# Windowed attention and a squared-ReLU MLP in one program: fp32 transposes, casting DMAs, hand-written engine orders, and products with V in 64-column array tiles

## The chip, the cores and the metric

The program runs on one core of one Trainium2 chip. The metric is device time in microseconds for one execution. TensorE (PE; its weight loads are shown as PEld), VectorE (DVE), ScalarE (ACT), GpSimd (POOL) and SyncE (SP) each run their own queue of instructions in order, and wait for each other through semaphores. DMA transfers are issued from a queue of SP, ACT or POOL.

## The reference

Attention over 8 batches, 8 heads, 576 positions and 64 values per head. A query sees the keys within 32 positions, and 8 global positions, drawn at random, see all and are seen by all. Its output, 4,608 tokens of 512 values, goes through two matrix products with a scaled and shifted squared ReLU between them.

```python
scores = scale * np.matmul(q, k.transpose(0, 1, 3, 2))
mask = np.abs(pos[:, None] - pos[None, :]) <= 32
mask = mask | is_global[:, None] | is_global[None, :]
scores = np.where(mask, scores, -1e9)
attn = softmax(scores)            # over the keys
x = np.matmul(attn, v)            # [8, 8, 576, 64] -> tokens [4608, 512]
r = np.maximum(x @ w_in, 0.0)     # w_in [512, 2048]
out = (s * (r * r) + b) @ w_out   # w_out [2048, 512]
```

## The kernel before

A batch's 576 positions are cut into five chunks of 120 (the last has 96); each chunk is filled to 128 rows with the 8 global positions. So a band of neighbouring chunks and the 8 globals cover everything a query can see, and a query that is global gets its sums from all five chunks (`gs`, and `finish_batch`, which writes its columns into `xt` at positions read from registers, one POOL copy per global, L398).

Heads are taken in pairs; pair p is heads 2hp and 2hp+1 of batch bi, with p = 4 bi + hp, so there are 32 pairs. For each pair: five transposes of K and five of Q (`trans_k`, `trans_q`) turn the natural rows into `kt` and into `qbufs`, where the two heads lie block-diagonally, with zeros in the other blocks. `qk` makes one score matrix per chunk for both heads at once, ScalarE takes its exponential, VectorE multiplies it with a mask. `pv` multiplies with V; `vbufs` holds 64 columns of V and 64 of ones beside them, so that a head's product has its output on partitions 0 to 63 and its row sums, 64 times over, on 64 to 127, and the two heads follow one another along the free dimension of `po`. `norm` takes the logarithm and the exponential of minus that (the reciprocal) on 64 partitions and 1,280 columns, and multiplies once per head.

The MLP runs in quanta of 0.9 us or so: a block of 512 tokens has 16 for the first product (4 weight tiles each, ReLU on ScalarE, square on VectorE) and 16 for the second. They are put between the attention steps by `Q`, eight per pair, as soon as a batch of attention is done; 32 quanta become due per batch and 64 after the last.

K, Q and V are loaded in fp32 by SP in halves of four heads (`load`, L124). The rows of the globals are gathered once for all batches by 24 DMAs on ACT's queue into a scratch in DRAM and copied from there into every chunk (`fill_globals`). Then casts to bf16 follow, on VectorE and POOL for batch 0 and on POOL afterwards (L285 to L287). The MLP weights are loaded in fp32 and cast, scaled by `s` and summed on POOL (`load_w`). PE's and SP's orders are as written; for ACT, DVE and POOL a scheduler of the framework sets the order:

```python
    ctx.enter_context(tc.manual_schedule(engines={ET.PE, ET.SP}))
```

Of the kernel before, what the change touches and what calls it, by code (L numbers as in the profile page):

```python
# [9 lines left out]
FP32 = mybir.dt.float32  # L10
# [22 lines left out]
W = [HI[c] - LO[c] for c in range(NCH)]  # L33

# [8 lines left out]

def halves(ap):

    return bass.AP(
        tensor=ap.tensor, offset=ap.offset,
        ap=[list(ap.ap[0]), [P, NCH], [HB + NG, 2], [1, HB]],
    )
# [3 lines left out]
def kernel(  # L53
# [14 lines left out]
    ctx.enter_context(tc.manual_schedule(engines={ET.PE, ET.SP}))  # L68
# [3 lines left out]
    natp = ctx.enter_context(tc.tile_pool(name="natp", bufs=1))  # L72
    castp = ctx.enter_context(tc.tile_pool(name="castp", bufs=2))
# [5 lines left out]
    mop = ctx.enter_context(tc.tile_pool(name="mop", bufs=3))  # L79
    dramp = ctx.enter_context(tc.tile_pool(name="dramp", bufs=1, space=bass.MemoryType.DRAM))  # L80
# [23 lines left out]
    nat = {}  # L104
    NATSRC = {"k": k, "q": q, "v": v}
    HG = 4

    def nat_tile(t, half):
        key = (t, half)
        if key not in nat:  # L110
            nat[key] = natp.tile([P, NCH, HG, D], FP32, tag=f"nat{t}{half}", name=f"nat{t}{half}")
        return nat[key]

    for t in ("k", "q", "v"):
        for half in range(2):
            nc.gpsimd.memset(nat_tile(t, half)[96:P, NCH - 1], 0.0)

    def load(bi, t, h0, nh):
        src = NATSRC[t]
        d = nat_tile(t, h0 // HG)  # L120
        a = h0 % HG
        for c in range(NCH):
            n = min(KC, S - KC * c)
            nc.sync.dma_start(  # L124
                out=d[0:n, c, a : a + nh],
                in_=src[bi, h0 : h0 + nh, KC * c : KC * c + n].rearrange("h s d -> s h d"),
            )

    gsc = {
        t: dramp.tile([B, NG, H, D], FP32, name=f"gsc{t}", tag=f"gsc{t}")  # L130
        for t in ("k", "q", "v")
    }

    def gather(eng, t, regs):
        for i in range(NG):
            eng.dma_start(
                out=gsc[t][:, i], in_=NATSRC[t][:, :, ds(regs[i], 1), :].rearrange("b h o d -> b (h o) d")
            )

    def fill_globals(eng, bi, t, half):  # L140
        d = nat_tile(t, half)
        src = gsc[t][bi, :, HG * half : HG * half + HG].rearrange("g h d -> g (h d)")
        src = bass.AP(
            tensor=src.tensor, offset=src.offset,
            ap=[list(src.ap[0]), [0, NCH], list(src.ap[1])],
        )
        eng.dma_start(
            out=d[KC:P].rearrange("p c h d -> p c (h d)"), in_=src
        )

    greg_a = [
        nc.scalar.value_load(g32[:1, i, 0:1], min_val=0, max_val=S - 1) for i in range(NG)
    ]
    greg_p = [
        nc.gpsimd.value_load(g32[:1, i, 0:1], min_val=0, max_val=S - 1) for i in range(NG)
    ]
    for t in ("k", "q", "v"):
        gather(nc.scalar, t, greg_a)

    for half in range(2):  # L160
        for t in ("k", "q", "v"):
            load(0, t, HG * half, HG)
            fill_globals(nc.scalar, 0, t, half)


    s_bc = const.tile([P, 1], FP32)
    nc.sync.dma_start(out=s_bc[:], in_=_bcast_dram(moe_s[:], P))
    b_bc = const.tile([P, 1], FP32)
    nc.sync.dma_start(out=b_bc[:], in_=_bcast_dram(moe_b[:], P))
    win_t = wpool.tile([P, 4, DF], BF16)  # L170
# [216 lines left out]
    def finish_batch(bi):  # L387
# [9 lines left out]
        for i in range(NG):  # L397
            nc.gpsimd.tensor_copy(  # L398
                out=xt[:, :, ds(greg_p[i], 1)], in_=xg[:, :, i : i + 1]
            )  # L400


    gts = {}
    gpb = {}

    def moe_quanta():
# [156 lines left out]
```

## Time and profile before

| | |
|---|---|
| median of 3 runs | 484.63 us (483.41 to 487.75) |
| the profiled execution | 487.77 us, with a span of 486.0 us from its first to its last instruction |
| PE, DVE, ACT, POOL busy | 73%, 60%, 47%, 27% of the span |
| first transpose; first product with V | 46.37 us; 68.76 us |
| ends of the batches' first and last `po` tiles | batch 0: 70 to 98 us; batch 7: 391 to 418 us |
| last stretch without attention | 424.2 to 486.0 us |
| DMA | 48.99 MB, mean 101 GB/s |

A row of a group reads: line, engine, operation, tiles out<-in, shapes, count; then total busy us and mean ns of one; then the idle time before these instructions and who ended it. In a timeline the first two numbers are the start and the duration in us, and a bracket gives the idle time before the row and its releaser. In the chain of waits the rows are start, duration and what ran. PEclk is the clock that TensorE was granted, as a share of full speed.

### The profile page before, as it was taken

To read this page: it belongs to the slowest core of one execution; us is meant where nothing else is said; L and a number is where in the kernel's file an instruction comes from. 1 tells how busy PE (TensorE), PEld (TensorE's weight loads), DVE (VectorE), ACT (ScalarE), POOL (GpSimd) and SP (SyncE) were. 2 spreads that over 40 slices of the span, in tenths; PEclk is the share of its full clock that TensorE was granted. 3 is DMA by queue.
4 is the path that set the end of the run, shared out by engine and by line. 5 is a ranking of instruction groups with operands and counts; after the bars stand their busy time and mean duration, and the time that the engine had idled before them with its cause. 6 is when DMAs were issued, how large, how long until landed. Compare 5 with 4: busy or idle time off the path is not lost.

```text
span 486.0 us, 7310 instructions
## 1 busy us (share of the span) xinstructions
PE 353.8 (73%) x2503; PEld 212.4 (44%) x2530; DVE 293.5 (60%) x672; ACT 230.8 (47%) x369; POOL 129.8 (27%) x155
## 2 busy tenths in 40 slices
PE   0000325558996897699969979996999599699996
PEld 0000113324553553366547537754765375354442
DVE  3902908849865865467758666775776476533331
ACT  1000115436844763387448645853865486352340
POOL 4334999934006200420241024024000100100000
PEclk9999999999997998799989998998999899989999
DMA  7999159999913105960990695199001000100102
GB/s 122 187 296 219 41 187 185 167 165 167 170 21 76 42 1 98 169 135 1 191 197 13 109 170 123 38 180 183 1 35 54 22 1 23 65 1 29 59 10 78
DMA packets 128149, 48.99 MB, mean 101 GB/s; under 512 B 117488, under 2 KB 119408, under 8 KB 128112
## 3 DMA queue, kind: packets, MB, share of 16 engines
q1 hardware_dynamic: 126096, 47.89, 50.7%
q10 hardware_dynamic: 2016, 0.64, 0.8%
q8 instruction: 20, 0.33, 0.3%
q14 instruction: 17, 0.14, 0.1%
HBM read 39.07 MB, written 9.83 MB: 101 GB/s over the span
## 4 chain that ended last, share of the span: by engine, by line
PE 34%; issue 26%; POOL 10%; DMA 10%; ACT 7%; SPq 6%; DVE 5%; ACTq 1%; POOLq 1%; DVEq 0%
PE psh L421 17%; PE pso L436 11%; SPq L124 5%; PE po L357 3%; ACT r L428 3%; POOL wout_t L470 2%; POOL xt L398 2%; DMA wi<-in_moe_w_in_dram 2%; ACT rep L374 2%; PE pss L334 2%; POOL wsum L477 2%; DMA wo<-in_moe_w_out_dram 2%; DVE xt L381 2%; POOL qb L286 2%; DMA natq<-in_q_dram 1%
## 5 line engine op out<-in xcount | busy, mean ns | idle before, releaser
L421 PE MATMUL psh<-xt,win_t 128*128 128x512 bf16 (+7 forms) x1020 | 155.7, 303 | 41.5 <-POOL xt L398 37.2
L436 PE MATMUL pso<-wout_t,g 128*128 128x512 bf16 x553 | 137.9, 382 | 4.7 <-DVE osb L443 3.3
L421 PEld LDWEIGHTS <-win_t 128*128 128x128 bf16 x1024 | 91.6, 103 | 95.4 <-issue 57.9
L428 ACT ACTIVATE r<-psh 128x512 bf16<-128x512 f32 x144 | 86.4, 600 | 87.3 <-PE psh L421 81.9
L338 ACT ACTIVATE e<-pss 128x384 bf16<-128x384 f32 (+1 forms) x160 | 73.4, 471 | 79.7 <-DMA wo<-in_moe_w_out_dram 49.5
L430 DVE TENSOR_TENSOR g<-r 128x512 bf16<-128x512 bf16 x144 | 70.6, 490 | 62.5 <-ACT r L428 62.1
L436 PEld LDWEIGHTS <-g 128*128 128x128 bf16 x576 | 55.6, 98 | 65.2 <-issue 10.1
L340 DVE TENSOR_TENSOR em<-e,mask 128x384 bf16<-128x384 bf16 (+1 forms) x160 | 73.1, 477 | 8.0 <-ACT e L338 6.9
L372 ACT ACTIVATE ln<-po 64x1280 f32<-64x1280 f32 x32 | 39.4, 1232 | 69.7 <-PE po L357 69.7
L334 PE MATMUL pss<-qbd,kt 128*128 128x384 bf16 (+1 forms) x160 | 55.1, 352 | 12.0 <-ACT e L338 9.9
L381 DVE TENSOR_TENSOR xt<-po,rep 64x600 bf16<-64x600 f32 x64 | 49.6, 775 | 16.3 <-ACT rep L374 14.8
L398 POOL COPY xt<-xg 128x4 bf16 x64 | 13.9, 217 | 145.0 <-DVE xt L381 102.7
L300 PE MATMUL pst<-ident,kb 128*128 128x128 bf16 x160 | 15.4, 232 | 48.3 <-DVE kb L285 46.4
L357 PE MATMUL po<-em,vx 128*128 128x160 bf16 (+3 forms) x448 | 35.7, 228 | 17.7 <-POOL vx L287 12.1
L285 POOL CAST kb<-natk 128x1280 bf16<-128x1280 f32 x14 | 18.0, 1284 | 100.4 <-DMA natq<-gscq 55.9
L374 ACT ACTIVATE rep<-ln 64x1280 f32<-64x1280 f32 x32 | 40.5, 1267 | 0.9
L443 DVE TENSOR_TENSOR osb<-pso,bias_row 128x512 f32<-128x512 f32 x36 | 24.7, 690 | 22.8 <-PE pso L436 22.5
L357 PEld LDWEIGHTS <-vx 128*128 128x128 bf16 x448 | 29.3, 101 | 19.5 <-POOL vx L287 12.3
L318 DVE COPY qbd<-pst 64x600 bf16<-64x600 bf16 x64 | 29.9, 466 | 11.8 <-PE pst L312 11.4
L300 PEld LDWEIGHTS <-kb 128*128 128x128 bf16 x160 | 12.2, 103 | 55.2 <-DVE kb L285 46.4
L375 DVE TENSOR_REDUCE gs<-po 128x16 f32<-128x80 f32 x32 | 7.7, 241 | 33.1 <-ACT ln L372 33.0
L334 PEld LDWEIGHTS <-kt 128*128 128x128 bf16 x160 | 16.5, 105 | 24.7 <-issue 12.1
(56 smaller groups left out, 190.3 us busy)
## 6 DMA issues: line engine op xcount, KB each, us to landing
out_dram<-osb SPq DMA_DIRECT2D x36, 256.0 KB
natk<-in_k_dram SPq DMA_DIRECT2D x64, 120.0 KB
natq<-in_q_dram SPq DMA_DIRECT2D x64, 120.0 KB
natv<-in_v_dram SPq DMA_DIRECT2D x64, 120.0 KB
wi<-in_moe_w_in_dram SPq DMA_DIRECT2D x4, 1024.0 KB
wo<-in_moe_w_out_dram SPq DMA_DIRECT2D x4, 1024.0 KB
natk<-in_k_dram SPq DMA_DIRECT2D x16, 96.0 KB
natq<-in_q_dram SPq DMA_DIRECT2D x16, 96.0 KB
```

What stands on the lines that cost most here:

```text
L318: nc.vector.tensor_copy(out=halves(qt[r, hh]), in_=ps[r].rearrange("p (c j) -> p c j", c=NCH)[:, :, 0:KC].rearrange("p c (a j) -> p c a j" ...
L334: nc.tensor.matmul(ps[:], kt[:, P * c : P * c + P], qt[:, :, LO[c] : HI[c]])
L338: nc.scalar.activation(e[:], ps[:], AF.Exp, scale=SCALE)
L340: nc.vector.tensor_mul(em[:], e[:], masks[c][:])
L357: nc.tensor.matmul(po[:, a : a + n], vx[:, c, 2 * hp + hh, :], emt[(p, c)][:, hh, lo - LO[c] : lo - LO[c] + n], start=bank not in started, ...
L372: nc.scalar.activation(ln[D:P], po[D:P], AF.Ln)
L374: nc.scalar.activation(rep[D:P], ln[D:P], AF.Exp, scale=-1.0)
L381: nc.vector.tensor_tensor(out=xt[D * hh : D * hh + D, hp].rearrange("p (c a j) -> p c a j", c=NCH, a=2), in0=halves(po[0:D, hh * LQ : hh * ...
L421: nc.tensor.matmul(psh[:, d0 : d0 + n], win_t[:, a, f * P : f * P + P], xts[bi][:, a, x0 : x0 + n], start=(a == 0 and j == 0), stop=(a == ...
L428: nc.scalar.activation(r[:], psh[:], AF.Relu)
L430: nc.vector.tensor_mul(g[:], r[:], r[:])
L436: nc.tensor.matmul(pso[:], gl[f][:, u * P : u * P + P], wout_t[:, f], start=(f == 0), stop=(f == 15),)
```

## The change

**Precision and layout of the inputs.** K and Q stay in fp32 and are transposed as fp32, with an fp32 identity. The copy out of PSUM makes the bf16. The eight rows of the globals now lie first in a chunk of K and V, and between the two halves of 60 in a chunk of Q, where `qbufs` has them, so that plain copies suffice. V and `w_in` are cast by the DMA that loads them, issued from POOL. `w_out` is copied to bf16 by ScalarE and its rows summed by VectorE, and `s` is applied when a tile is stored. K, Q and V have two buffers, each for all eight heads.

**Globals of batch 0.** They don't come through DRAM any more: fp32 products with a selection matrix take them out of the loaded rows (`select_globals`, `select_v`). The gathers for the other batches are issued from POOL after pair 0 and pair 1.

**Order.** All five engines' orders are as written. A pair has eight slots. VectorE's part of a slot is put off to the next one (`later`), and the normalising of a pair is done in slots 1 and 3 of the next pair. `finish_batch` comes in slot 5 of the next batch's first pair and is issued in slot 6. Batch 0 runs without quanta, then 14 quanta go beside `weights_out`, then batch 1 has three quanta per pair and each later batch 8 per pair; six quanta of a block are always left over when the next block becomes due.

**Products with V.** `pv` writes the products of the two heads to partitions 0 to 63 and 64 to 127 of the same columns, with 64 columns of weights each: first the V columns of both heads (`part` 0), then the ones (`part` 1). So the row sums of both heads stand on 128 partitions in 640 columns, and there is one logarithm, one exponential and one multiply per pair at 128 partitions. There are 28 products per pair where there were 14.

```diff
-    ctx.enter_context(tc.manual_schedule(engines={ET.PE, ET.SP}))
+    ctx.enter_context(
+        tc.manual_schedule(engines={ET.PE, ET.SP, ET.Activation, ET.DVE, ET.Pool})
+    )
...
+    def load_v(bi):
+        d = vbufs[bi % 2]
+        for c in range(NCH):
+            n = min(KC, S - KC * c)
+            nc.gpsimd.dma_start(
+                out=d[NG : NG + n, c, :, 0:D],
+                in_=v[bi, :, KC * c : KC * c + n].rearrange("h s d -> s h d"),
+            )
+
+    load_k(nc.sync, 0, 0, HG)
+    load_q(nc.scalar, 0, 0, HG, 0)
+    load_q(nc.sync, 0, 0, HG, 1)
+    load_v(0)
...
+    for j in range(4):
+        nc.gpsimd.dma_start(
+            out=win_t[:, :, 512 * j : 512 * j + 512],
+            in_=w_in2[:, :, 512 * j : 512 * j + 512],
+        )
...
+    def tr(ps, dst0, src, c, hp):
+        nc.tensor.transpose(
+            ps[:, dst0 : dst0 + P], src2(src)[:, c, P * hp : P * hp + P], identf[:]
+        )
...
+    def trans_a(p):
+        bi, hp = divmod(p, 4)
+        ps = ps_s.tile([P, 512], FP32, tag="s", name="pst")
+        for c in range(4):
+            tr(ps, P * c, natk[bi % 2], c, hp)
+        kt = ktp.tile([P, LQ], BF16, tag="kt", name="kt")
+        ktile[p] = kt
+        nc.scalar.copy(out=kt[:, 0:512], in_=ps[:])
...
+        for i, (src, sel) in enumerate(((natk[0], selk), (natq[0], selq))):
+            for c in range(NCH):
+                nc.tensor.matmul(
+                    ps[:, i], src2(src)[:, c, P * hp : P * hp + P], sel[:, c],
+                    start=(c == 0), stop=(c == NCH - 1),
+                )
...
     def pv(p):
         bi, hp = divmod(p, 4)
-        vx = vbufs[bi % NV]
+        vx = vbufs[bi % 2]
         po = ps_o.tile([P, 2 * LQ], FP32, tag="o", name="po")
         started = set()
-        for hh in range(2):
+        for part in range(2):
             for c in range(NCH):
...
+                for a, n, x in pieces(part * LQ, c):
+                    for hh in range(2):
+                        key = (a // 512, hh)
+                        nc.tensor.matmul(
+                            po[D * hh : D * hh + D, a : a + n],
+                            vx[:, c, 2 * hp + hh, D * part : D * part + D],
+                            emt[(p, c)][:, hh, x : x + n],
+                            start=key not in started, stop=(part == 1 or c == NCH - 1),
+                            skip_group_check=True,
+                        )
+                        started.add(key)
...
-        nc.scalar.activation(ln[D:P], po[D:P], AF.Ln)
...
+            nc.scalar.activation(ln[:], po[:, LQ : 2 * LQ], AF.Ln)
...
+        for s in range(8):
+            prev, later[:] = list(later), []
+            if s < NCH:
+                qk(p, s)
+                if s in (1, 3, 4):
+                    step()
+            elif s == 5:
+                if hp == 0 and bi > 0:
+                    later.append(lambda: finish_batch(bi - 1))
+                if trans_next:
+                    trans_a(p + 1)
+            elif s == 6:
+                if trans_next:
+                    trans_b(p + 1)
+                    if bi == 0:
+                        select_globals(p + 1)
+            else:
+                if p == 0:
+                    select_v()
+                pv(p)
+                pending.extend(norm_steps(p))
+            for f in prev:
+                f()
+            Q(nq[s])
...
+    for p in range(4):
+        run_pair(p, Z, p < 3)
+        if p == 0:
+            gather(k, gsk)
+            gather(q, gsq)
+        if p == 1:
+            gather(v, gsv)
...
+            load_v(1)
+            prefetch_hw(1)
...
+        nq = [1] * 8 if bi > 1 else [0, 1, 0, 1, 0, 1, 0, 0]
```

Three places show how the instructions stand. On TensorE, in batch 0, from the last transpose ahead of pair 0's product with V before; `vx_401` is V with its ones, `em` the masked exponentials:

```order
L312 MATMUL pst<-ident,qb 128x128
L357 LDWEIGHTS vx_401
L357 MATMUL po<-em_527,vx_401 128x160
L357 LDWEIGHTS vx_401
L357 MATMUL po<-em_533,vx_401 128x192
```

And at the same place now, for pair 1, with the selecting products (`psg`) between:

```order
L349 MATMUL pst<-identf,natk_98 128x128 x4
L349 MATMUL pst_508<-identf,natk_98 128x128
L349 MATMUL pst_508<-identf,natq_100 128x128
L349 MATMUL pst<-identf,natq_100 128x128 x4
L391 MATMUL psg<-selk,natk_98 128x8 x5
L391 MATMUL psg<-selq,natq_100 128x8 x5
L450 LDWEIGHTS vx_102
L450 MATMUL po<-em_471,vx_102 64x160
L450 LDWEIGHTS vx_102
L450 MATMUL po<-em_471,vx_102 64x160
```

Each chunk has two products of 64 rows where it had one of 128, the transposes read the loaded fp32 tiles, and an fp32 product stands without a load row of its own.

On POOL, at the start before, where `qbd` are the tiles of `qbufs` and the casts of the weights follow them:

```order
L275 MEMSET qbd_405 64x640
L276 MEMSET qbd_405 64x640
L275 MEMSET qbd_408 64x640
L276 MEMSET qbd_408 64x640
L275 MEMSET qbd_411 64x640
L276 MEMSET qbd_411 64x640
L465 CAST win_t<-wi 128x4x512 x4
```

And now, of POOL's start, the issues and the last register load ahead of them:

```order
L170 DMA vx_102<-in_v_dram 120x8x64 x4
L170 DMA vx_102<-in_v_dram 96x8x64
L194 DMA win_t<-in_moe_w_in_dram 128x4x512 x4
L206 TENSOR_LOAD gidx_i_96
L206 ISA x2
...
L301 MEMSET qbd_104 64x640
L302 MEMSET qbd_104 64x640
```

The clearing of `qbufs` has moved behind nine DMA issues and eight register loads.

On TensorE at the end of batch 2, where the first product of a new MLP block (`psh`) reads the last columns of `xt`, before:

```order
L357 MATMUL po<-em_1978,vx_401 128x160
...
L436 LDWEIGHTS g_1777
L436 MATMUL pso<-wout_t,g_1777 128x512
L334 LDWEIGHTS kt
L334 MATMUL pss<-qbd_405,kt 128x320
L421 LDWEIGHTS win_t
L421 MATMUL psh<-xt,win_t 128x128
```

And now, in slots 4 to 6 of batch 3's first pair:

```order
L423 MATMUL pss<-qbd_104,kt 128x320
...
L349 MATMUL pst<-identf,natk_99 128x128 x4
...
L533 LDWEIGHTS g_1878
L533 MATMUL pso<-wout_t,g_1878 128x512
L349 MATMUL pst_2129<-identf,natk_99 128x128
L349 MATMUL pst_2129<-identf,natq_101 128x128
L349 MATMUL pst<-identf,natq_101 128x128 x4
L518 LDWEIGHTS win_t
L518 MATMUL psh<-xt,win_t 128x128
```

Two quanta and one score stood between the last product with V and the new block; now a whole pair's scores, its transposes and six quanta do.

More of the change, by code (lines that the diff above doesn't have):

```diff
@@ L102 @@
     g32 = gidx_i64[:].bitcast(mybir.dt.int32).rearrange("p (a b) -> p a b", b=2)
[L104 to L149, printed above, removed]
@@ L262 @@
[L262 to L274 removed]
+        if c in (0, NCH - 1):
+            nc.vector.tensor_copy(
+                out=gadd[:, WIN + HB : WIN + HB + NG], in_=view(vkey[:, c : c + 1], [0, NG])
+            )
@@ L479, in bias @@
+    flush()
+    while pending:
+        step()
+        flush()
+    finish_batch(0)
+    quanta[0] = 32
+    for j in range(4):
+        Q(3)
+        weights_out(j)
+        flush()
+    Q(2)
+    flush()
+    trans_a(4)
+    trans_b(4)
+    flush()
     def bias():
```

569 lines of the change are left out of this document (316 added, 253 removed).

## The prediction

> **What bounds the kernel now.** I read the page's span and busy shares, then the time by stage, then one batch's end, the groups by line, and last the start.
>
> ```profile
> span 486.0 us, 7310 instructions
> PE 353.8 (73%) x2503; PEld 212.4 (44%) x2530; DVE 293.5 (60%) x672; ACT 230.8 (47%) x369; POOL 129.8 (27%) x155
> ```
>
> The shares average over very different stages, so the windows come next: up to the first product with V, batch 0's pairs, batch 1, six equal batches, the tail (engine columns are us busy and instructions).
>
> ```profile
> core 0: us, PE busy (x) PEld busy (x) DVE busy (x) ACT busy (x) POOL busy (x), PEclk, DMA share, GB/s
> 0.00:68.80 68.80, 4.88 (x26) 2.49 (x27) 31.02 (x66) 3.52 (x6) 40.25 (x39) 1.00 0.71 168
> 68.80:106.10 37.30, 19.00 (x104) 11.14 (x105) 26.27 (x47) 17.15 (x24) 28.99 (x23) 1.00 1.13 187
> 106.10:151.80 45.70, 38.05 (x240) 20.50 (x245) 32.84 (x74) 27.11 (x44) 10.82 (x15) 0.98 0.70 106
> 151.80:424.20 272.40, 234.03 (x1820) 150.66 (x1838) 184.18 (x445) 163.93 (x263) 49.71 (x79) 0.94 0.45 86
> 424.20:486.00 61.80, 57.87 (x315) 27.65 (x318) 19.16 (x40) 19.11 (x32) 0.00 (x0) 0.94 0.09 35
> ```
>
> For 106 us TensorE does little. Then six batches take 272.4 / 6 = 45.4 us each with PE busy 86%; no other engine passes 68%. So time there is TensorE time plus its holes. One hole stands at each batch's end:
>
> ```profile
> 199.21 1.56 DVE L381 TENSOR_TENSOR xt<-po,rep 64x600 bf16<-64x600 f32 x2
> 200.84 2.20 POOL L398 COPY xt<-xg 128x4 bf16 x8 [5.23 <-DVE xt L381]
> 203.09 1.76 PE L421 MATMUL psh<-xt,win_t 128*128 128x384 bf16 x7 [4.58 <-POOL xt L398]
> ...
> 201.10:207.80 6.70, 4.71 (x21) 2.68 (x21) 1.03 (x4) 1.87 (x4) 5.23 (x11) 0.50 1.16 171
> ```
>
> PE waits 4.58 us for the last `xt` columns and then runs 6.7 us at clock 0.50. The price without holes comes from the tail, whose second block (32 quanta) runs at full clock:
>
> ```profile
> 454.65 7.99 PE psh L421 x37
> 462.69 5.77 PE psh L421 x26
> 468.46 4.96 PE pso L436 x23
> 473.48 8.81 PE pso L436 x40
> 482.31 0.69 DVE osb L443
> ```
>
> That is 482.3 - 454.65 = 27.7 us, 0.87 per quantum.
>
> **The change, part by part.** First TensorE, per pair of heads:
>
> ```profile
> 194.18 0.44 PE L300 MATMUL pst<-ident,kb 128*128 128x128 bf16 x5
> 194.46 1.03 PE L436 MATMUL pso<-wout_t,g 128*128 128x512 bf16 x4
> 222.17 0.83 PE po L357 x14
> 98.11 0.55 PEld L481 LDWEIGHTS psb<-wsum,onesf 128*128 128x128 f32 x2
> L481 PEld LDWEIGHTS psb<-wsum,onesf x2: 333/335/337, 98.1 to 98.3; 128*128 128x128 f32 x2
> ```
>
> Five bf16 transposes hold TensorE 194.46 - 194.18 = 0.28 us, so ten cost 0.56; the 14 products with V cost 0.83 for 1,792 columns, and the scores, with as many columns, about 0.8. Check: 27.7 + 4 x 2.2 + 4.6 wait + about 3.4 for half clock = 44.5, near 45.4.
>
> The fp32 transpose isn't in the trace. Its nearest row is the only fp32 load: two loads take 0.55 us together and one lasts 0.335, so the second began 0.215 after the first. I take one such load per transpose: 10 x 0.215 = 2.15 us, plus 1.6 per pair. Ends: the bf16 spacing (0.56), and two loads each as that fp32 product has (4.3). [...]
>
> The 28 products with 64 output columns: if the two heads run side by side, 0.83; if one after another, 28 x 0.83/14 = 1.66. I take the middle, 1.25. [...]
>
> The hole: the last pair's normalising moves into the next batch's first pair, beside six quanta left over from the old block (5.2 us at 0.87). The sums, their quotient and the POOL copies (2.2 us) follow the fifth score; TensorE has a quantum and six transposes meanwhile. I leave 1.5 us of wait per batch (between 0 and 4.6) and no half clock. Per batch: 27.7 + 4 x (0.8 + 2.15 + 1.25) + 1.5 = 46.0, against 45.4: six batches **+3.6 us**.
>
> The other engines:
>
> ```profile
> L372 ACT ACTIVATE ln<-po 64x1280 f32<-64x1280 f32 x32 | 39.4, 1232 | 69.7 <-PE po L357 69.7
> L374 ACT ACTIVATE rep<-ln 64x1280 f32<-64x1280 f32 x32 | 40.5, 1267 | 0.9
> L381 DVE TENSOR_TENSOR xt<-po,rep 64x600 bf16<-64x600 f32 x64 | 49.6, 775 | 16.3 <-ACT rep L374 14.8
> L338 ACT ACTIVATE e<-pss 128x384 bf16<-128x384 f32 x96 | 47.0, 492 | 19.5 <-PE pss L334 15.8 <-DVE em L340 3.4
> L340 DVE TENSOR_TENSOR em<-e,mask 128x384 bf16<-128x384 bf16 x96 | 50.3, 542 | 6.4 <-ACT e L338 5.6
> L428 ACT ACTIVATE r<-psh 128x512 bf16<-128x512 f32 x144 | 86.4, 600 | 87.3 <-PE psh L421 81.9 <-DVE g L430 2.4 <-PE pst L300 0.3
> L430 DVE TENSOR_TENSOR g<-r 128x512 bf16<-128x512 bf16 x144 | 70.6, 490 | 62.5 <-ACT r L428 62.1
> L318 DVE COPY qbd<-pst 64x600 bf16<-64x600 bf16 x64 | 29.9, 466 | 11.8 <-PE pst L312 11.4
> ```
>
> Logarithm and exponential at half the elements per partition fall from 2.5 to about 1.3 us per pair, and a copy of K (512 columns, like the 0.6 us row of L428) comes to ScalarE; VectorE loses one of two 0.775 multiplies. Neither engine bounds the six batches, so this counts at nothing there: PE covers it, and with that cover gone it would be a gain. POOL loses its casts and issues V's loads instead; K, Q and V now have two buffers each and are loaded two and a half pairs ahead of their first use. SyncE issues 18 loads per batch instead of 36, of the same bytes, and the stores queue behind them; with the DMA share at 0.45 in the six batches I cost that at nothing, and if a load came late, TensorE would wait for it in the transposes at the end of a batch. The scale `s` moves from the weights into the VectorE instruction that adds the bias row anyway: nothing, by the same idle VectorE time.
>
> Now the start:
>
> ```profile
> 8.37 0.29 POOL masks.py:199 TENSOR_SCALAR_AFFINE_SELECT ident<-ident 128x128 bf16<-128x128 bf16 x1 [5.47 <-issue]
> 8.79 2.24 POOL L269 MEMSET vx<- 128x2560 bf16 x1
> 12.89 1.59 SPq L124 DMA_DIRECT2D natk<-in_k_dram  x2
> ...
> 46.37 0.71 PE L300 MATMUL pst<-ident,kb 128*128 128x128 bf16 x5 [46.37 <-DVE kb L285]
> 68.69 5.44 POOL L470 TENSOR_SCALAR wout_t<-wo,s_bc 128x2048 bf16<-128x2048 f32 x1
> 68.76 1.68 PE L357 MATMUL po<-em,vx 128*128 128x160 bf16 x14 [12.07 <-POOL vx L287]
> ```
>
> Before, TensorE waits 46 us for a cast that needs the gathered rows, and 12 more for a V cast behind the weights on POOL. Both go. Late next is POOL, which now clears `qbufs`, which the first score reads, only behind the issues of V and `w_in` and the register loads. Its queue: 7,680 cleared elements at 2.24/2560 = 6.7 us, small ones to about 8.3; nine DMA issues at 1.3 (an SP issue of 480 rows takes 0.8, V's have 960; POOL issues none in this trace, so 0.5 to 5.4, the last being the scaling on POOL) = 11.7; register loads 5.5; two clears of 640 elements 1.1: first score at **27 us** (19 to 65).
>
> Batch 0 then goes pair by pair: scores bound by ScalarE, 5 x 0.49 + 1.3, about 4 us; transposes 2.15; ten fp32 selecting products, two loads each, 4.3; V about 2: 12.4, three times, and 6 for the last pair: 43. Normalising, quotient and copies 5.5: 76. Fourteen quanta with the conversion of `w_out` on ScalarE, 14 x 0.6 + 4 x 2.0 (1232 / 1280 = 0.96 ns per element, 2,048 elements), 3 for its third chunk, which is loaded late, and 2.5 for transposes: 98. Batch 1 has three quanta per pair; VectorE carries 5 x 0.54 for the masks, about 1.8 for the copies (four times the 0.466 row at half to full length), 0.8 and 3 x 0.49, 6.8 us per pair; with hand-overs I take 8: 130. There before stands at 151.8, but six quanta (5.2) further: **-17 us**. The gathers (24 issues) move to POOL's queue behind pair 0, with batch 0's last copies behind them: 31 us at 1.3, then 4.5 for clearing the second V buffer and 6.5 for five loads: done by about 72, ahead of 76, but close.
>
> The tail is the same 64 quanta. Its first block takes 454.65 - 424.2 = 30.4 after a hole like the others, its second 27.7; with the hole short: **-2.8**. Sum: 486.0 - 17 + 3.6 - 2.8 = 469.8. The profiled execution took 487.77 with its span of 486.0, so this gives 471.6, which is 16.2 less. From the median of the runs, 484.63, that is **468**.
>
> **Rivals.**
>
> Fast TensorE: transposes at half the fp32 load's spacing (1.1 us for ten) or at the bf16 one (0.56). For it: a transpose only moves data, where L481 multiplies, and the load row is of a product. Per pair 1.05 to 1.6 less, 24 pairs, 25 to 38, and with side-by-side products 10 more: 443 down to 420.
>
> Slow array halves (slower): the 28 loads of 64 columns don't hide, and each product pays the 0.103 that a load row lasts:
>
> ```profile
> L421 PEld LDWEIGHTS <-win_t 128*128 128x128 bf16 x1024 | 91.6, 103 | 95.4 <-issue 57.9
> ```
>
> 28 x 0.103 = 2.9, plus 1.65 per pair and 40 in six batches: 508. It decides once transposes and V together pass 3.4 + 16.2/24 = 4.1 us per pair.
>
> Double transposes: two loads each, plus 2.15 per pair on 28 pairs, about 60: 528.
>
> POOL's issues: at 4 to 5.4 us each the first score moves to 51 to 65, 24 to 38 later: 492 to 506.
>
> **Chances.** Forecast 0.42, fast TensorE 0.27, slow halves 0.13, POOL 0.11, double transposes 0.07. The range that leaves out the ends of the first and the whole of the last: 426 to 506. A measurement here tells about 1% (480 to 489). Faster: 0.27 and three quarters of 0.42, 0.58; slower: most of the slow three and a little of the forecast, 0.30; same 0.12.
>
> **What would show it.** Right: first `pss` row near 27 us; PE waits for `xt` under 2 us and clock 1.00 across the batch ends; ten transposes in about 2.2 us; V's 28 products in 0.8 to 1.7. Wrong: a PE wait on POOL's `qbd` near 50 us, two fp32 load rows per transpose, or a batch over 50 us.

## The result, and the profile after

The changed kernel takes 437.86 us (median; 437.15 to 439.33), beside 486.19 for the kernel before: a ratio of 0.9015, with an interval of 0.8958 to 0.9071. That is 48 us less where 16 were forecast. The profiled execution took 437.67 us with a span of 436.0.

The page of the changed kernel and its windows: up to the first product with V, to the first MLP product, to pair 8's first score, six batches, the rest; then the four pairs of a batch, cut at the logarithm, which comes in slot 1 of the next pair.

```profile
PE 387.0 (89%) x3063; PEld 241.8 (55%) x3063; DVE 265.6 (61%) x650; ACT 206.7 (47%) x405; POOL 84.5 (19%) x162
...
0.00:32.50 32.50, 17.63 (x70) 13.51 (x70) 18.46 (x50) 4.58 (x8) 23.04 (x35) 1.00 1.29 171
32.50:72.67 40.17, 27.51 (x187) 19.77 (x188) 21.68 (x56) 11.99 (x25) 22.24 (x34) 1.00 0.89 130
72.67:124.04 51.37, 41.65 (x289) 21.90 (x288) 36.59 (x84) 29.46 (x51) 6.01 (x13) 0.97 0.70 114
124.04:372.40 248.36, 240.35 (x2179) 157.90 (x2180) 166.75 (x417) 141.59 (x289) 31.61 (x73) 1.00 0.67 91
372.40:436.00 63.60, 59.82 (x341) 28.69 (x339) 22.13 (x45) 19.10 (x32) 1.62 (x8) 1.00 0.11 42
...
178.70:189.00 10.30, 10.13 (x109) 7.35 (x108) 7.78 (x21) 7.75 (x18) 0.00 (x0) 1.00 1.90 146
189.00:198.90 9.90, 9.73 (x91) 6.25 (x90) 6.74 (x18) 6.13 (x14) 0.00 (x0) 1.00 0.60 100
198.90:208.70 9.80, 9.80 (x77) 5.54 (x75) 6.03 (x14) 3.95 (x9) 0.00 (x0) 1.00 0.14 55
208.70:220.10 11.40, 10.39 (x95) 7.03 (x93) 7.50 (x19) 5.59 (x13) 6.00 (x13) 1.00 0.59 113
```

A steady batch takes 41.4 us, with PE busy 97% of it (before: 45.4 on average, 44.2 to 44.9 in most and 50.0 in the first). Stage by stage against before: up to the six batches 124.0 instead of 151.8 (27.8 less, but with six quanta, 5.2 us, still owed); six batches 248.4 instead of 272.4 (24.0 less); the tail 63.6 instead of 61.8 with the six quanta in it. The two starts of the six batches aren't the same instruction: 124.0 is pair 8's first score, and 151.8 is the first product behind the wait, 4.9 us after pair 8's first score of that kernel (146.9). In the last four rows a batch's second pair stands first and its first pair last: that one holds the old batch's end.

The timeline of PE over one of those batches, with four transposes, the products with V and the batch's end:

```profile
192.01 0.60 PE L349 MATMUL pst<-identf,natk 128*128 128x128 f32 x4
192.44 1.04 PE L518 MATMUL psh<-xt,win_t 128*128 128x128 bf16 x8
...
195.32 1.04 PE L450 MATMUL po<-em,vx 128*64 128x160 bf16 x28
196.29 1.04 PE L533 MATMUL pso<-wout_t,g 128*128 128x512 bf16 x4
...
214.02 0.25 PE L518 MATMUL psh<-xt,win_t 128*128 128x192 bf16 x1
215.28 0.95 PE L518 MATMUL psh<-xt,win_t 128*128 128x320 bf16 x7 [1.01 <-POOL xt L498]
216.16 1.03 PE L450 MATMUL po<-em,vx 128*64 128x160 bf16 x28
```

Four fp32 transposes hold TensorE 192.44 - 192.01 = 0.43 us, so ten cost 1.09 (forecast 2.15). The 28 products with V hold it 0.97 (forecast 1.25; the 14 before 0.83). PE waits 1.01 us for `xt` (forecast 1.5; before 4.58), and the clock stays at 1.00 across all batch ends. With 0.87 per quantum and 0.8 for the scores, TensorE's own work is 8 x 0.87 + 0.8 + 1.09 + 0.97 = 9.8 us per pair: the third pair shown takes just that, the others 0.1 to 1.6 more.

The start, from the same timeline:

```profile
8.46 4.57 POOL L170 DMA_DIRECT2D vx<-in_v_dram  x5
...
13.01 3.02 POOL L194 DMA_DIRECT2D win_t<-in_moe_w_in_dram  x4
...
18.82 0.62 POOL L301 MEMSET qbd<- 64x640 bf16 x1 [2.79 <-issue]
...
20.18 0.74 PE L423 MATMUL pss<-qbd,kt 128*128 128x320 bf16 x2 [4.04 <-POOL qbd L302]
...
69.35 3.27 POOL L498 COPY xt<-xg 128x4 bf16 x8 [10.73 <-DVE xg L496]
...
72.67 7.58 PE L518 MATMUL psh<-xt,win_t 128*128 128x512 bf16 x24 [6.35 <-POOL xt L498]
```

The first score comes at 20.2 us (forecast 27), and PE does wait there for POOL's clears, but by 0.4 us only: VectorE's last copies for that score end at 19.76. 24 products of 512 columns take 7.58 us from 72.67 on; from 77.3 on a product takes half as long as ahead of it (starts 0.216 us apart instead of 0.427).

### The profile page after: what moved, and what is told of

It reads as the page before. It is cut to its first block, busy times and chain, and to the rows that moved or that the text cites. A ratio compares the mean times of both kernels' runs of the same rounds, so it can differ in the third digit from the quotient of the medians.

```text
span 436.0 us, 8254 instructions
## 1 busy us (share of the span) xinstructions
PE 387.0 (89%) x3063; PEld 241.8 (55%) x3063; DVE 265.6 (61%) x650; ACT 206.7 (47%) x405; POOL 84.5 (19%) x162
## 4 chain that ended last, share of the span: by engine, by line
issue 49%; PE 30%; POOL 10%; ACT 5%; DVE 4%; POOLq 1%; DMA 1%; ACTq 0%; DVEq 0%
PE psh L518 10%; PE pso L533 10%; POOL vx L170 4%; POOL xt L498 3%; PE psg L391 3%; PE po L450 3%; PE pst L349 2%; ACT e L427 1%; ACT r L525 1%; PE pss L423 1%; DMA wo<-in_moe_w_out_dram 1%; POOL vx L124 1%; ACT kt L363 1%; POOLq L206 1%; DVE vx L417 1%
## 5 line engine op out<-in xcount | busy, mean ns | idle before, releaser
L518 PEld LDWEIGHTS <-win_t 128*128 128x128 bf16 x1024 | 86.8, 98 | 62.6 <-issue 21.3
L423 PE MATMUL pss<-qbd,kt 128*128 128x384 bf16 (+1 forms) x160 | 51.4, 337 | 12.1 <-POOL qbd L302 4.0
L542 DVE SCALAR_TENSOR_TENSOR osb<-pso,s_bc,bias_row 128x512 f32<-128x512 f32 x36 | 26.9, 747 | 31.8 <-PE pso L533 31.8
L381 DVE CAST qbd<-pst 64x512 bf16<-64x512 f32 x64 | 44.1, 689 | 2.1 <-PE pst L349 1.2
L450 PE MATMUL po<-em,vx 128*64 128x160 bf16 (+3 forms) x896 | 37.1, 233 | 3.1 <-DVE vx L417 1.7
L450 PEld LDWEIGHTS <-vx 128*64 128x64 bf16 x896 | 29.7, 117 | 14.5 <-issue 7.9
L349 PE MATMUL pst<-identf,natk 128*128 128x128 f32 x160 | 30.0, 295 | 8.7 <-DMA natk<-in_k_dram 8.6
L170 POOL DMA_DIRECT2D vx<-in_v_dram x40 | 35.3, 897 | 3.2 <-issue 3.2
L349 PE MATMUL pst<-identf,natq 128*128 128x128 f32 x160 | 28.8, 298 | 5.7 <-ACT kt L363 4.8
L349 PEld LDWEIGHTS pst<-identf,natk 128*128 128x128 f32 x160 | 20.9, 150 | 18.7 <-POOL identf masks.py:199 8.6
L481 DVE TENSOR_TENSOR xt<-po,rep 128x600 bf16<-128x600 f32 x32 | 25.1, 783 | 8.6 <-ACT rep L479 8.6
L363 ACT CAST kt<-pst 128x512 bf16<-128x512 f32 x32 | 20.1, 629 | 18.2 <-PE pst L349 18.2
```

Of the source, the lines that this page charges most:

```text
L170: nc.gpsimd.dma_start(out=d[NG : NG + n, c, :, 0:D], in_=v[bi, :, KC * c : KC * c + n].rearrange("h s d -> s h d"),)
L349: nc.tensor.transpose(ps[:, dst0 : dst0 + P], src2(src)[:, c, P * hp : P * hp + P], identf[:])
L381: nc.vector.tensor_copy(out=qdst(p, hh, 0, 512), in_=ps[r])
L423: nc.tensor.matmul(ps[:], ktile[p][:, P * c : P * c + P], qbufs[p % 3][:, :, LO[c] : HI[c]])
L450: nc.tensor.matmul(po[D * hh : D * hh + D, a : a + n], vx[:, c, 2 * hp + hh, D * part : D * part + D], emt[(p, c)][:, hh, x : x + n], star ...
L518: nc.tensor.matmul(psh[:, d0 : d0 + n], win_t[:, a, f * P : f * P + P], xts[bi][:, a, x0 : x0 + n], start=(a == 0 and j == 0), stop=(a == ...
```

## The experiments

Two theories stood against each other. The first: the holes at the batch ends carried most of the gain, and the rest of the change costs TensorE a little. The second: the gain is in the precision, the array tiles and the start. In the text below a batch is given by the time from one logarithm to the next for each of its pairs, the first pair first. The hole is PE's wait for `xt` at a batch's end with the half clock that comes with it, and carried quanta are those of an old MLP block that are left over for that place.

### The hole alone, in the kernel before

```diff
+    hold = [0]
     def Q(n=1):
         for _ in range(n):
-            if moe_left[0] > 0:
+            if moe_left[0] > hold[0]:
...
+        hold[0] = 6 if bi == 1 else 0
         if hp == 0:
```

> The kernel before with one thing from the change: batch 1 runs 26 quanta instead of 32, so that six quanta of the old MLP block are left over whenever a new block becomes due, and one more batch of them in the tail. Nothing else is changed, and nothing is left out. Theory (the holes at the batch ends carried most of the gain): seven holes of 4.6 us wait and about 3.4 us of half clock, of which about 1 us stays: 7 x 7 = 49 less, 484.6 - 49 = about 436, and the half clock after 108 us is gone. Rival (the gain is in the precision, the array tiles and the start, and a hole only moves: in the first pair of a batch ScalarE and VectorE have the old quanta and the normalising at once, and PE waits for them instead): under half of it, 462 to 485.

446.33 us, ratio 0.9157 (0.9105 to 0.921): 40 of the 48 us with this one edit. The windows of a batch's pairs:

```profile
265.00:274.10 9.10, 9.05 (x63) 5.09 (x62) 7.02 (x20) 4.75 (x8) 3.12 (x9) 1.00 1.15 183
274.10:284.30 10.20, 9.42 (x95) 8.10 (x93) 7.88 (x19) 8.88 (x15) 3.92 (x3) 1.00 1.09 172
284.30:294.50 10.20, 9.42 (x94) 8.02 (x93) 8.95 (x24) 8.89 (x15) 2.50 (x2) 1.00 0.47 119
294.50:303.60 9.10, 9.05 (x61) 5.01 (x62) 6.34 (x16) 4.77 (x8) 0.00 (x0) 1.00 0.09 30
```

This batch takes 38.6 us, about 6 less than like batches before (44.2 to 44.9), and 2.8 less than in the changed kernel. So the carried quanta alone shorten a batch by more than the whole change does; the other parts together, among them the order written by hand for ScalarE, VectorE and POOL, make it longer again. Not all holes closed: at one batch end the wait moved to another place, where VectorE, ordered by the scheduler, normalised before it emptied the MLP's tile:

```profile
185.97 1.57 PE L436 MATMUL pso<-wout_t,g 128*128 128x512 bf16 x3 [4.97 <-DVE osb L443]
```

That pair took 15.9 us instead of 9.0; it makes up most of the distance to the 436 expected.

### The hole put back, in the changed kernel

```diff
-        nq = [1] * 8 if bi > 1 else [0, 1, 0, 1, 0, 1, 0, 0]
+        nq = [1] * 8 if bi > 1 else [[1, 0, 1, 0, 1, 1, 0, 1], [0, 1, 0, 1, 0, 1, 0, 1]][hp // 2]
         if bi > 1 and hp == 0:
+            flush()
+            while pending:
+                step()
+                flush()
+            finish_batch(bi - 1)
...
-                if hp == 0 and bi > 0:
-                    later.append(lambda: finish_batch(bi - 1))
```

> The changed kernel with the hole put back: batch 1 runs the six quanta too (18 instead of 12), and the normalising of the last pair and finish_batch come at a batch's end, ahead of the next batch's first score. Nothing is left out. Theory (a hole costs about 7 us, as in the kernel before): seven holes, 437.9 + 49 = about 487, PE waits for xt of 4 to 5 us, each with a stretch of half clock behind it. [...] If carrying were worth nothing: 438.

467.61 us, ratio 0.9623 (0.9553 to 0.9693): 29.7 more than the changed kernel, where the theory had 49. The wait and the clock are those of the theory all the same. PE's timeline at a batch's end, and the window of the stretch behind:

```profile
217.12 0.25 PE L518 MATMUL psh<-xt,win_t 128*128 128x192 bf16 x1
221.52 1.70 PE L518 MATMUL psh<-xt,win_t 128*128 128x320 bf16 x7 [4.16 <-POOL xt L498]
...
219.70:226.50 6.80, 4.98 (x23) 3.31 (x23) 1.32 (x4) 1.96 (x4) 5.79 (x12) 0.50 1.34 189
```

The wait is back at 4.16 us with half clock behind it, for 6.8 us at some ends and 3.4 at others. PE works for 5.0 of the 6.8 us shown, so the half clock costs about 2.5 us there beside the wait (an estimate: half of that work), and less at the others. A batch takes 46.0 us, 4.6 more. The first pair lost 7 to 8, and the three others were 2.9 shorter together; how much of that is only the logarithm's earlier place, I have not separated.

### Eight quanta left over instead of six

```diff
-        nq = [1] * 8 if bi > 1 else [0, 1, 0, 1, 0, 1, 0, 0]
+        nq = [1] * 8 if bi > 1 else ([0, 1, 0, 1, 0, 1, 0, 0] if hp < 2 else [0, 1, 0, 0, 0, 1, 0, 0])
```

> The changed kernel with eight quanta left over at a batch's end instead of six (batch 1 runs ten instead of twelve, the tail two more). Theory (the 1.0 us wait for xt that stays at each batch's end is the rest of the hole): six or seven times 1.0 to 1.4, about 429 to 432. Rival (the first pair of a batch is held by ScalarE and VectorE, which do the last pair's normalising beside the scores): 437 to 439.

433.78 us, ratio 0.8918 (0.8863 to 0.8974): the first pair of a batch takes 10.2 us instead of 11.4 and waits for `xt` no more. The theory holds, a little short of its 429 to 432; 4.1 us were left in the changed kernel at this place.

### The price of the transposes

Each transpose twice from pair 8 on, and, in the kernel before, the fp32 product whose loads priced the forecast, issued again in a batch's middle:

```diff
-            tr(ps, P * c, natk[bi % 2], c, hp)
+            tr(ps, P * c, natk[bi % 2], c, hp, 1 + (p > 7))
...
+        if p == 14:
+            psx = ps_m.tile([P, DM], FP32, tag="moe", name="psx")
+            for _ in range(4):
+                nc.tensor.matmul(psx[:], onesf[:], wsum[:])
```

> The kernel before, with the fp32 product that makes the bias row's sum (the one whose load rows priced the forecast's transposes) issued four times more ahead of pair 14's products with V, into a tile that nobody reads. If 0.215 us from one fp32 load to the next is what a load costs, its rows here stand as far apart, and the loads last 0.33. If that row was read in a stretch where TensorE ran at half speed (the clock's record of the kernel before begins only at 108.9 us, and 14 products with V take 1.68 us at 68.8 and 0.98 later), the two loads of a product stand about 0.108 apart here and last 0.2 or less.

The load rows of that product at 229.6 us, by the timeline and by its line:

```profile
229.57 0.30 PEld L526 LDWEIGHTS psx<-wsum,onesf 128*128 128x128 f32 x2
...
L526 PEld LDWEIGHTS psx<-wsum,onesf x8: 190/190/192, 229.6 to 232.3; 128*128 128x128 f32 x8
```

Two loads take 0.30 us together and one lasts 0.190, so they stand 0.110 apart. At 98.1 us the same two take 0.55 and one lasts 0.335: 0.215 apart. The forecast had read its price at half speed. (The run took 489.86 us; only its rows are used.)

> The changed kernel with each fp32 transpose issued twice from pair 8 on, 240 more in 24 pairs; the second writes the same again. Theory (full-clock price read from the trace after, 0.109 us each, all of it on the path): 240 x 0.109 = 26, so about 464. The forecast's price (0.215 each): 240 x 0.215 = 52, about 490. If TensorE is not the bound of the six batches: about 438.

451.31 us, ratio 0.9286 (0.9225 to 0.9346). Eight transposes now hold PE from 193.53 to 194.40, 0.109 each:

```profile
193.53 1.04 PE L350 MATMUL pst<-identf,natk 128*128 128x128 f32 x8
194.40 1.04 PE L519 MATMUL psh<-xt,win_t 128*128 128x128 bf16 x8
```

But a batch grew only from 41.4 to 43.9 us, 2.5 of the 4.4 that 40 transposes hold TensorE. By pairs: 11.4, 11.0, 10.7, 10.9 instead of 11.4, 10.3, 10.0, 9.8. In the last pair, which has no ReLU and takes just TensorE's own time, all of it counts; in the pair with the batch's end, none.

K and Q as bf16, cast by their DMA (batches 1 to 7), with bf16 transposes:

```diff
-        load_k(nc.sync, bi, 0, H)
-        load_q(nc.sync, bi, 0, H, 0)
-        load_q(nc.sync, bi, 0, H, 1)
+        load_k(nc.gpsimd, bi, 0, H)
+        load_q(nc.gpsimd, bi, 0, H, 0)
+        load_q(nc.gpsimd, bi, 0, H, 1)
...
-            ps[:, dst0 : dst0 + P], src2(src)[:, c, P * hp : P * hp + P], identf[:]
+            ps[:, dst0 : dst0 + P], src2(src)[:, c, P * hp : P * hp + P],
+            (identb if src.dtype == BF16 else identf)[:],
```

> The changed kernel with K and Q of batches 1 to 7 cast to bf16 by the DMA that loads them, issued from POOL like V, and transposed as bf16 (batch 0 stays as it is). Nothing is left out. The run with doubled transposes showed that of 1.09 us more per pair the first pair of a batch feels nothing, the next two 0.7, the last 1.1. Theory from that: half of it back, (0 + 0.7 + 0.7 + 1.1) / 2 = 1.2 per batch, six batches 7.5: about 430. By the forecast's price (2.15 against 0.56 for ten): 24 x 1.6 = 38, about 400. Rival (15 more casting loads per batch, 0.9 us each on POOL's queue, come late, and TensorE waits for them in the transposes): 440 or more.

434.63 us, ratio 0.8938 (0.8882 to 0.8993). Pairs of 11.3, 10.0, 9.7, 9.3 us: 1.1 less per batch, as worked out. VectorE's copies out of PSUM are shorter here too (0.42 us instead of 0.69), which this run doesn't separate from the transposes. About 5 us were lost once, in batch 1, whose last pair took 12.1 us instead of 7.3 for the loads of batch 2; so the total misses the 430:

```profile
122.16 0.71 PE L353 MATMUL pst<-identb,bq 128*128 128x128 bf16 x5 [4.03 <-DMA bq<-in_q_dram]
```

### The array tiles

One head's products after the other's:

```diff
-        for part in range(2):
+        for part, hh in ((0, 0), (0, 1), (1, 0), (1, 1)):
             for c in range(NCH):
                 for a, n, x in pieces(part * LQ, c):
-                    for hh in range(2):
```

> The changed kernel with the 28 products with V in another order: first all of one head, then all of the other, for V and then for the ones, so that neighbours in TensorE's queue write the same half of the array's columns. Nothing is left out. Theory (0.97 us for 28 is so little because the halves of a neighbouring pair run side by side): the products take about 1.7 us per pair, 0.7 more; from the doubled transposes, where 1.09 more per pair gave 0, 0.7, 0.7 and 1.1 over a batch's pairs, this gives about 1.6 per batch, and more in the first two batches: 447 to 452. Rival (each product is quick for its 64 columns of weights, in any order): 438.

447.43 us, ratio 0.9188 (0.9118 to 0.9258).

```profile
188.94 1.39 PE L450 MATMUL po<-em,vx 128*64 128x160 bf16 x28
190.26 1.05 PE L518 MATMUL psh<-xt,win_t 128*128 128x128 bf16 x8
```

The 28 products hold PE 1.32 us instead of 0.97, and every pair is 0.3 to 0.4 longer. Order matters, and the halves do run side by side in the changed kernel: by the single rows of its trace the two heads' products start 0.003 us apart (195.415 and 195.418, 195.497 and 195.500). The price is half of the 0.7 expected; the total lies in the expected range by luck, because all of it counted, 1.5 us per batch. By the single rows of this run, matched to the queue by their widths, the second head's first product begins at 189.200, ahead of the last three of the first head's seven (189.264, 189.292, 189.324), though it stands behind them in the queue: the halves overlap over some distance.

Now the tiles undone in the changed kernel, with the wide normalising, and then the reverse: the tiles put into the kernel before with its carried quanta (the same lines the other way).

```diff
-                            po[D * hh : D * hh + D, a : a + n],
-                            vx[:, c, 2 * hp + hh, D * part : D * part + D],
+                        po[:, a : a + n], vx[:, c, 2 * hp + hh, :],
...
-            nc.scalar.activation(ln[:], po[:, LQ : 2 * LQ], AF.Ln)
+            nc.scalar.activation(ln[D:P], po[D:P], AF.Ln)
```

> The changed kernel with the products with V as before: 14 products with 128 columns of weights (64 of V, 64 of ones), the heads one after another in po, logarithm and exponential on 64 partitions and 1,280 columns, two multiplies per pair. Nothing is left out. Theory (the two heads of the array tiles run side by side at full pace, so TensorE gains and loses nothing, and ScalarE and VectorE don't bound the six batches): within 1% of 437.9. First rival (the array tiles cost TensorE 0.1 to 0.8 us per pair, as the forecast's 1.25 for 0.83 had it): 28 pairs x 0.1 to 0.42, 426 to 435. Second rival (VectorE and ScalarE bound the first two batches, and get 0.8 and 1.0 us more per pair; the longer chain also delays xt at a batch's end): 445 or more.

491.43 us, ratio 1.009 (1.0059 to 1.0121): the whole gain is gone, 53.6 us. The theory and the first rival missed. The second rival came true in the two places that it named: pair 8's first score comes 15.0 us later, and `xt` comes late at every batch end. It did not name the pairs in a batch's middle. The windows of a batch, the second pair first, one batch end, and PE's waits for ScalarE at the transposes, over five batches, here and then in the changed kernel:

```profile
204.10:215.80 11.70, 10.31 (x94) 7.26 (x93) 8.45 (x22) 9.21 (x16) 0.00 (x0) 1.00 1.47 158
215.80:227.20 11.40, 9.96 (x77) 6.22 (x76) 7.37 (x19) 7.68 (x13) 0.00 (x0) 1.00 0.20 31
227.20:237.30 10.10, 9.72 (x62) 5.53 (x62) 6.71 (x15) 5.28 (x9) 0.00 (x0) 1.00 0.14 52
237.30:252.20 14.90, 11.64 (x80) 8.26 (x80) 8.86 (x21) 6.84 (x11) 6.00 (x13) 0.89 0.67 103
...
197.73 1.25 PE L526 MATMUL psh<-xt,win_t 128*128 128x384 bf16 x7 [3.23 <-POOL xt L506]
...
PE pst L349 <- ACT e L427: 6.4, 10, 0.6
PE pst L349 <- ACT kt L363: 5.3, 10, 0.5
...
PE pst L349 <- ACT kt L363: 1.7, 10, 0.2
```

ScalarE has 1.3 to 1.6 us more per pair and VectorE 0.6 to 0.7 (1.4 in the first). The second and the third pair, which have the ReLUs, take 1.4 to 1.5 us longer: PE waits there for ScalarE's exponential and its copy of K, 1.2 us per pair where it was 0.2. The first pair takes 3.5 us longer, since the longer chain from logarithm to `xt` outlasts the six quanta: PE waits 3.23 us, and a stretch of half clock follows at every batch end. A batch takes 48.0 us, 6.6 more.

> The kernel before with the six quanta left over and with the array tiles: 28 products with V, two heads side by side in po, one logarithm, one exponential (128 partitions, 640 columns) and one multiply per pair. K, Q, V, the weights and the order stay as before. Theory (the two pairs of a batch with the first MLP product take 10.2 us instead of 9.0 because ScalarE carries eight ReLUs, five exponentials and 2.5 us of normalising there): they fall to 9.1 to 9.4, so about 2 per batch, six batches 12 to 14, about 433. Rival (the wide normalising in the changed kernel cost so much only because of the order written by hand there): 443 to 447.

433.22 us, ratio 0.8914 (0.8851 to 0.8976): as expected in sum, and 4.6 us below the changed kernel. Its pairs with ScalarE's eight ReLUs:

```profile
261.90:271.50 9.60, 9.54 (x110) 8.15 (x109) 8.20 (x20) 7.80 (x15) 2.93 (x3) 1.00 1.04 180
271.50:281.10 9.60, 9.54 (x110) 8.15 (x109) 7.49 (x22) 7.80 (x15) 2.59 (x2) 1.00 0.37 106
```

They take 9.6 instead of 10.2, with 1.1 us less on ScalarE, and now PE is busy all of it; the two others grew by 0.3. So a batch goes from 38.5 to 37.8 by its logarithms, and only 0.7 comes from there, not 2: the sum came right by luck. Of the 13.1 us, 7.8 lie ahead of batch 2 and 1.8 at the one batch end that had kept its hole. The same part is worth 0.7 per batch here and 6.6 in the changed kernel. So for the batches the rival's reason may hold, that the order written by hand makes it dear there; the two kernels differ in more than that order, and no run separates it.

### The start

Products that nobody reads, in TensorE's idle time up to the first MLP product:

```diff
+    def warm(n):
+        if n:
+            ps = ps_m.tile([P, 512], FP32, tag="moe", name="psw")
+            for _ in range(n):
+                nc.tensor.matmul(ps[:], hot[:, 0:P], hot[:])
...
+    warm(14)
     trans_a(0)
     trans_b(0)
     select_globals(0)
+    warm(18)
...
+                if bi == 0:
+                    warm(1)
```

> The changed kernel with extra products of TensorE whose result nobody reads, in its idle time up to the first MLP block: 14 before the first transposes, 18 after the first selecting products, one behind each score of batch 0, 10 and 6 ahead of the first and the last product with V, 28 before the first quanta. Theory (all of TensorE's work up to 77 us runs at half speed because it is idle so often): transposes, selecting products and V take half, about 4 us per pair, and the first quanta too, 437.9 - 14 = about 424. Rival (batch 0 goes by the loads, by VectorE's 6 us per pair and by ScalarE, and the extra products stand in the way): 434 to 445.

427.45 us, ratio 0.879 (0.8734 to 0.8845).

```profile
63.95 5.34 PE L526 MATMUL psh<-xt,win_t 128*128 128x512 bf16 x24 [0.20 <-POOL xt L506]
```

The first MLP products start at 63.95 instead of 72.67, and 24 of them take 5.34 us instead of 7.58. Pairs 1 and 2 take 7.7 to 7.9 us instead of 11.4. The clock's record begins at 4.3 us instead of 77.2, with full clock from 21.3 to 52.1. So up to 77 us the changed kernel runs TensorE at half speed, and filling its idle time changes that: 28 products with V hold TensorE 1.74 us there at 47.3, and 0.97 here at 42.9. 10.4 of the expected 14 came.

### Joined

The edits of the runs with added products and with eight quanta together, and then those with the bf16 transposes and batch 2's loads issued early:

> The changed kernel with the extra products of TensorE up to 64 us and with eight quanta left over. The two alone gave 427.5 and 433.8 beside 437.9; they act in different places, so the theory adds them: 437.9 - 10.4 - 4.1 = about 423.4. Rival (a shorter start only moves the wait for the loads of batch 2): 425 to 428.

422.59 us, ratio 0.87 (0.8632 to 0.8768): the two add up.

```diff
     finish_batch(0)
+    prefetch_hw(2)
     quanta[0] = 32
```

> The one before with K and Q of batches 1 to 7 cast by their DMA and transposed as bf16, and batch 2's loads issued from POOL ahead of the first quanta (in the run with bf16 alone TensorE waited for them, the last pair of batch 1 took 12.1 us instead of 7.3). Theory: another 6 x 1.1 for the transposes and 4 to 5 for the wait that doesn't come back: 423.4 - 6.6, about 417, to 413 if batch 1 gets shorter too. Rival (POOL's casting loads hold the first batches back): 423 or more.

424.73 us, ratio 0.8731 (0.8671 to 0.8791): a miss. The batches are as expected (38.6 us, pairs of 9.6, 10.0, 9.7, 9.3), but PE waits at the first MLP product; by the waits of that stretch:

```profile
POOL xt L513 <- DVE kt L390: 20.7, 1, 20.7
...
PE psh L533 <- POOL xt L513: 10.0, 1, 10.0
```

```diff
             load_v(1)
-            prefetch_hw(1)
...
     finish_batch(0)
-    prefetch_hw(2)
+    prefetch_hw(1)
...
+    prefetch_hw(2)
     trans_a(4)
```

> The kernel of the run before, in which the casting loads of batches 1 and 2 are issued from POOL behind the copies that finish batch 0, and those of batch 2 behind the weights, instead of ahead of them. In that run TensorE waited 10.0 us for POOL's xt copies, which stood behind 15 loads in POOL's queue, and later for w_out. Theory (only the place in POOL's queue cost it): the wait goes, 424.7 - 10 = 414 to 415, and the first pair of batch 1 starts by 86 us instead of 100. Rival (the casting loads take so much of the DMA engines that the first batch's transposes or w_out are late wherever they are issued): 420 or more.

412.59 us, ratio 0.8481 (0.8442 to 0.8519). The wait for POOL is gone, and batch 1's first score comes at 88.9 us instead of 100.2. The place in POOL's queue had cost it. It isn't the 86 expected: PE still waits 6.7 us once, up to 82.1, where ScalarE and VectorE wait 4.5 and 6.9 us for the load of `w_out`, as the rival had it. This is the fastest of the kernels: 25 us less than the changed one, 74 less than before.

## Why the prediction was wrong

Faster was right, and 437.9 lies in the range (426 to 506); the size was not. By stages of the forecast's sum: pair 8's first score came at 124.0, not 130 (6.0 less); six batches took 41.4 each, not 46.0 (27.6 less); the tail 63.6, where the sum left 469.8 - 130 - 276 = 63.8. Together 33.8, which is 469.8 - 436.0. Of a batch's 4.6, the transposes are 4.2, the products with V 1.1 and the hole 0.5, and about 1.3 was lost again, because the pairs take that much more than TensorE's own time and the hole, which the sum put at nothing. (The sum set its 130 against 151.8, a point 4.9 us behind pair 8's first score before, so its first step holds one wait of a batch's end.)

**The transposes failed, and through the row that priced them.** The step took 0.215 us per transpose from two loads at 98.11. That row is at half speed. The same product at 229.6 has its loads 0.110 apart, and the transposes of the changed kernel 0.109: ten cost 1.09, not 2.15, 4 x 1.06 = 4.2 us per batch. The sign was among the forecast's own rows: 14 products with V took 1.68 us at 68.76 and 0.83 at 222 (0.98 as the timeline counts). The clock column could not show it: the trace's record of the clock begins at 108.9, and the column says 1.00 ahead of that. The case that came true is the first rival, fast TensorE (443 down to 420), with its dearer price for the transposes. Its reason did not come true: a transpose takes as long as that product's load (0.109 beside 0.110), so the row was the right one, read at the wrong clock.

**Adding up TensorE's time failed in part.** The run with doubled transposes has the forecast's own price, 2.18 us for what ten transposes do, and takes 451 us, not 470: only 2.5 of its 4.4 us per batch count.

**The products with V: right in kind, mis-sized.** 0.97 instead of 1.25, another 1.1 us per batch. The truth lies near the lower end of 0.83: the heads run side by side, and a different order costs 0.35 us per pair. As a price of the halves the trace shows at most 0.14 us per pair, 0.97 against 0.83; slow halves did not come.

**The hole: right.** 1.5 us of wait and no half clock were forecast; 1.0 and none came. By the forecast's own terms the kernel before with carried quanta takes 27.7 + 4 x 2.2 + 1.5 = 38.0 per batch, and 38.6 was measured. The forecast's check of the old price was loose: it put the half clock at 3.4 us, half of 6.7, but PE works for 4.7 of these, so the same halving gives 2.4. What the forecast did not say is that this one edit takes more off a batch than the whole change does, about 5.8 us against 2.9, from 44.3 in a like batch before. By TensorE's own time the new transposes and products put back 4 x (0.53 + 0.14) = 2.7, about the difference, but the runs don't show that this is the account: bf16 transposes brought back 1.1 of it, two more carried quanta 1.2, and the tiles shortened a batch of the kernel before by 0.7.

**"PE covers it" failed.** Narrower normalising was costed at nothing, since neither ScalarE nor VectorE bounds the six batches; a gain was allowed for only with that cover gone. Undone in the changed kernel, together with the tiles, it costs 6.6 us per batch and 53.6 in all; added to the kernel before with carried quanta, it gives 0.7 and 13.1. The mean shares hid two places: the pairs with ReLUs, where ScalarE holds PE up well before it is full (9.2 of 11.7 us), and the batch's end, where the chain through `ln`, `rep` and `xt` has to fit behind six quanta. The forecast did name that chain, but with its new length, and gave the narrowing no part in the hole's closing.

**The start: the mechanism right, the terms too big.** POOL's clears are what the first score waits for, though by 0.4 us only, at 20.2 instead of 27: V's five loads are issued in 4.57 us and `w_in`'s four in 3.02, 0.84 each instead of 1.3, and the queue loses 2.8 us, not 5.5, ahead of the clears. The pairs of batch 0 took 11.4 (forecast 12.4) because the same half-speed row was right there (five transposes hold TensorE 1.12 us at 22.6); batch 1's took 7 instead of 8. Keeping TensorE busy there was worth 10.4 us in the run with added products.

## What to carry to other kernels

Before a row prices a step, look at what a known operation costs next to it: here 14 products took 1.68 us there and 0.98 elsewhere in the same view, and the row was at half speed, though the clock column said 1.00. A mean busy share says nothing of cover: cut the window into the units that differ (here, pairs with and without ReLUs, and the one with the batch's end) before an engine's work is costed at nothing. Leaving a few quanta of independent work over at a boundary gave 40 us by itself in the kernel before, and it needs a chain short enough to fit behind them: PE waited 1.0 us with the changed kernel's chain and 3.23 with the longer one. What a part is worth depends on the kernel around it: the tiles with the narrower normalising were worth 53.6 us in one and 13.1 in the other.

## What the runs showed of the hardware

The profile's clock record begins at 77.2 us in the changed kernel and at 108.9 before, and the column reads 1.00 ahead of that, while products run at half speed (in the changed kernel the first MLP products start 0.427 us apart up to 76.9, and 0.216 apart from 77.5 on). In the six batches waits of 1.0 us in the changed kernel, and of 1.5 in the run with K and Q as bf16, leave the clock alone; waits of 3.23 us (the run with the products with V as before) to 5.15 (the kernel before) came with 3.4 or 6.8 us at half clock. So did a shorter one: in the changed kernel a wait of 2.2 us that ended at 93.9, the second above 2 us within five, came with 3.4. And in the run with one head's products after the other's, a product for the second half of the array's columns was recorded as starting ahead of three that stand before it in TensorE's queue and use the first half (189.200 against 189.264 and later), so there the starts were not in the queue's order.
